# One of three wide additions a unit by an accumulating DMA, and VectorE's order in a unit redone

## The chip, the cores and the metric

The kernel runs on one core of one Trainium2 chip. The metric is the device time of one execution in microseconds; the median of several executions is compared. TensorE multiplies matrices, VectorE and ScalarE work element by element, GpSimd and SyncE (SP) here mostly issue DMAs. Lines such as L427 are lines of the kernel before.

## The reference

A layer-normalised input `x` (2048 tokens of 512) goes two ways: through attention with 32 heads over cached keys and values of 2048 positions, and through a small network B that gates the result. What matters here is the attention:

```python
q = (xn @ wq).reshape(B, Sq, H, Dh)                  # H = 32, Dh = 128, Sq = 2048
scores = einsum("bhqd,bhkd->bhqk", q, k_cache) * Dh ** -0.5
p = softmax(scores, axis=-1)
o = einsum("bhqk,bhkd->bhqd", p, v_cache)
s = o.reshape(B, Sq, H * Dh) @ wo
g = silu(B_ref(xn, ...))
return x + s * g
```

The softmax needs, for every query, the sum of its 2048 exponentials. Those sums are what the change is about.

## The kernel before

The attention is cut into 128 units: 8 groups of 4 heads, 4 blocks of 512 queries, and the 4 heads within. A unit is one head and 512 queries, and it is walked through in 8 slots (`p` = 0 to 7) of two blocks of 128 keys each. The last unit, 127, is written out by hand at the end. The order on every engine is the program's order (`pin`); nothing is moved by a scheduler. The main loop runs over slots, `n = 8 u + p`; one pass over `p` for a given `u` is called the body of unit `u` here.

- `s_slot` (L405): two score matmuls into a PSUM tile `ps_s` and one exponential of 128x1024 on ScalarE (L416) into half of a tile `pT`. A unit fills four `pT` tiles of 128x2048 (pT[0] to pT[3]) in bf16. Six such buffers exist.
- `pv_slot` (L437) multiplies `pT` with the values into `ps_o`, ten slots behind the scores; there are two buffers of `ps_o`.
- The sums over keys: VectorE adds the four `pT` tiles, keys still on partitions. `add_first` (L419, slot 4) makes acc = pT[0] + pT[1]; `add_next` (L425) adds pT[2] in slot 6 and pT[3] in slot 0 of the next body. These are the three wide additions of 128x2048. `fold` (L429) and `fold_last` (L433) halve acc twice, to 128x512.
- `turn` (L458, slot 3 of the next body) transposes acc by a DMA on SP's queue into `tT`, so that queries lie on partitions. `turned_sums` (L462, slot 0 of the body after that) reduces `tT` on VectorE, takes the reciprocal, and issues the DMA `dr` to DRAM; `bcast` (L471, slot 1) issues the DMA `rb`, which reads `dr` and spreads it over all partitions.
- `norm` (L476), called by `norm_queue` in slot 7 of the body two units later, multiplies `ps_o` by `rb` on VectorE into `oT`; this frees `ps_o`.
- `wo_mm` and `wo_post` (L500, L533) multiply `oT` with the output weights into the one bank `ps_wo` and add it to `sacc` on VectorE (L549; in the last group also L558 and L560).
- For units 16 to 123 the query projection is made for two heads at once by seven products instead of eight (`product`, L363; `q_part`, L383). `q_part` reads the products from the one bank `ps_q` on VectorE, in slots 3 and 6, and TensorE's next products into the bank come after it.

SP's queue issues, in this order within a body, `dr`, `rb`, `turn`, and then the loads of keys (`load_k`), values (`load_v`) and weights for later groups. GpSimd computes only small statistics before the attention starts and issues no DMA.

Of the kernel before, what the change touches and what calls it, by code (L numbers as in the profile page):

```python
# [9 lines left out]
ALU = mybir.AluOpType  # L10
FP32 = mybir.dt.float32
BF16 = mybir.dt.bfloat16
# [5 lines left out]
def kernel(  # L18
# [15 lines left out]
    nc = tc.nc  # L34
    P = nc.NUM_PARTITIONS
# [26 lines left out]
    pin = tc.keep_in_program_order  # L62

    def pool(name, bufs=1, space=None, **kw):
        if space is not None:
            kw["space"] = space
        return tc.tile_pool(name=name, bufs=bufs, **kw)
# [43 lines left out]
    def mm(out, lhsT, rhs, start, stop, **kw):  # L111
# [9 lines left out]
        out=ident[:], in0=diag[:], scalar1=0.0, scalar2=None, op0=ALU.is_equal))  # L121
# [6 lines left out]
    NU = len(units)  # L128
    TURN = range(NU - HG)
    NS = NU * SPU  # L130
    kTs, vBs, wqs, wos, oTs, st = {}, {}, {}, {}, {}, {}
# [183 lines left out]
    def q_mm(u, dcs, tag="xa"):  # L315
        g, qt, hh = units[u]
        if dcs[0] == 0:
            st[u] = dict(psq=psX.tile([P, 512], FP32, tag=tag, name="ps_q"))
        for dc in dcs:
            mm(st[u]["psq"][:], wqs[g * HG + hh][:, dc, :],  # L320
               xnT[:, dc, qt * 512:(qt + 1) * 512], dc == 0, dc == DC - 1)
# [83 lines left out]
    def s_slot(u, p):  # L405
        g, qt, hh = units[u]
        s = st[u]
        sps = psS.tile([P, 2, 512], FP32, name="ps_s")
        for j in range(2):
            kc = 2 * p + j  # L410
            kv = kTs[g * HG + hh].rearrange("d (i p j) -> d i j p", p=P, j=KJ)
            mm(sps[:, j, :], kv[:, kc // KJ, kc % KJ, :], s["qT"][:], True, True)
        if p % 2 == 0:
            s.setdefault("pT", []).append(pB.tile([P, 4, 512], BF16, tag="pT", bufs=6, name="pT"))
        jj = 2 * (p % 2)
        pin(nc.scalar.activation(  # L416
            out=s["pT"][-1][:, jj:jj + 2, :], in_=sps[:], func=ACT.Exp, scale=SCALE))

    def add_first(u):  # L419
        s = st[u]  # L420
        s["acc"] = pB.tile([P, 4, 512], BF16, tag="acc", bufs=2, name="acc")
        pin(nc.vector.tensor_tensor(  # L422
            out=s["acc"][:], in0=s["pT"][0][:], in1=s["pT"][1][:], op=ALU.add))

    def add_next(u, i):  # L425
        a = st[u]["acc"]
        pin(nc.vector.tensor_tensor(out=a[:], in0=a[:], in1=st[u]["pT"][i][:], op=ALU.add))  # L427

    def fold(u):  # L429
        a = st[u]["acc"]  # L430
        pin(nc.vector.tensor_tensor(out=a[:, 0:2, :], in0=a[:, 0:2, :], in1=a[:, 2:4, :], op=ALU.add))  # L431

    def fold_last(u):  # L433
        a = st[u]["acc"]
        pin(nc.vector.tensor_tensor(out=a[:, 0, :], in0=a[:, 0, :], in1=a[:, 1, :], op=ALU.add))  # L435
# [22 lines left out]
    def turn(u):  # L458
        st[u]["tT"] = pB.tile([P, 4, P], BF16, tag="tT", bufs=2, name="tT")
        pin(nc.sync.dma_start_transpose(out=st[u]["tT"][:], in_=st[u]["acc"][:, 0, :]))  # L460

    def turned_sums(u):  # L462
        s = st[u]
        sm = smp.tile([P, 4], FP32, name="sm")
        pin(nc.vector.tensor_reduce(out=sm[:], in_=s["tT"][:], axis=mybir.AxisListType.X, op=ALU.add))  # L465
        rc = smp.tile([P, 4], FP32, name="rc")
        pin(nc.vector.reciprocal(out=rc[:], in_=sm[:]))
        s["dr"] = drp.tile([P, 4], FP32, name="dr")
        pin(nc.sync.dma_start(out=s["dr"][:], in_=rc[:]))

    def bcast(u):  # L471
        st[u]["rb"] = pB.tile([P, 512], FP32, tag="rb", bufs=2, name="rb")
        pin(nc.sync.dma_start(
            out=st[u]["rb"][:], in_=st[u]["dr"][:].rearrange("p j -> (p j)").partition_broadcast(P)))

    def norm(u):  # L476
        g, qt, hh = units[u]
        s = st.pop(u)
        if hh == 0:
            oTs[(g, qt)] = pB.tile([P, HG, 512], BF16, tag="oT", bufs=2, name="oT")  # L480
        o, rb, to = s["o"][:], s["rb"][:], oTs[(g, qt)][:, hh, :]
        if u in TURN:
            o = o.rearrange("k (j p) -> k p j", j=4)
            rb, to = (x.rearrange("k (p j) -> k p j", j=4) for x in (rb, to))
        pin(nc.vector.tensor_tensor(out=to, in0=o, in1=rb, op=ALU.mult))  # L485
# [23 lines left out]
    def fin_load(t):  # L509
        xl = token(False, "xl")  # L510
        pin(nc.sync.dma_start(out=xl[:], in_=xsrc[t]))
        fin[t] = xl
# [16 lines left out]
    def pay():  # L529
        while owed:  # L530
            y_out(*owed.popleft(), nc.sync)
# [276 lines left out]
    pB = left.enter_context(pool("pB", reuse_waits="tile"))  # L808
# [40 lines left out]
    def pv_run(n):  # L849
        while pv_at[0] <= n - LAG:  # L850
            pv_slot(*divmod(pv_at[0], SPU))
            pv_at[0] += 1

    def norm_queue(u):
        norm(u)
        gg, qq, hh = units[u]
        if hh == HG - 1:
            wo_todo.extend((gg, 4 * qq + ts) for ts in range(4))
            if gg == NG - 1 and qq not in LATE:
                fin_load(4 * qq)  # L860

    UA, UB = NU - 2, NU - 1

    def wo_slot(part, n, each=2, **kw):
        gg, t = wo_todo[0]
        if part < HG // each:
            wo_mm(gg, t, tuple(range(part * each, (part + 1) * each)), **kw)
            return
        wo_todo.popleft()
        wo_post(gg, t, n)  # L870
        if gg == NG - 1 and t % 4 < 3 and t + 1 not in fin and t // 4 not in LATE:
            fin_load(t + 1)

    FIRST, LAST = 16, NU - 4
    pairs = range(FIRST, LAST + 1, 2)
    q_plan = defaultdict(list)
    steps = defaultdict(list)
    for v in pairs:
        a = (v - 2) * SPU
# [5 lines left out]
    def run_steps(n, which):  # L885
        for fn, v, k in steps.get(n, ()):
            if fn is which:
                fn(v, k)
# [4 lines left out]
    for h in range(HG, H, 2):  # L893
        u = (h // HG) * QT * HG + (-4, -2)[h % HG // 2]
# [8 lines left out]
    for n in range(UB * SPU):  # L903
        u, p = divmod(n, SPU)
        extra = len(wo_todo) > 1 and u in (2 * HG, 2 * HG + 1)
        if p == 0 and wo_box:
            wo_slot(4, n, each=1)
        s_slot(u, p)
        pv_run(n)
        for v, dcs in q_plan.get(n, ()):  # L910
            q_mm(v, dcs)
        run_steps(n, product)
        if p == 0 and u - 2 in TURN:
            turned_sums(u - 2)
        if p == 1 and u - 2 in TURN:
            bcast(u - 2)
        if p == 0 and 1 <= u:
            add_next(u - 1, 3)
            fold(u - 1)
            if u != UA:  # L920
                fold_last(u - 1)
        if p == 3 and u - 1 in TURN:
            turn(u - 1)
        if p == 0:
            twice = extra
        if twice and p < 3:
            wo_slot(p, n, tag="xa")
        for v, k in ((u + 1, 3), (u + 2, 7)):
            if p == k and "psq" in st.get(v, ()) and (k == 3) == (v > FIRST):
                q_copy(v)  # L930
        if p == 3:
            run_steps(n, q_part)
        if u - 2 in TURN:
            norm_p, sum_p, wo_p, each = 7, 5, 3, 1
        else:
            norm_p, sum_p, wo_p, each = 4, 5, 4, 1
        at_wo = [wo_p + i for i in range(HG // each + 1)]
        if FIRST - 2 <= u < LAST:
            at_wo = ([0, 3, 4, 6, 7], [0, 2, 3, 6, 7], [3, 4, 5, 6, 7], [0, 2, 3, 6, 7])[u % 4]
        if p == norm_p and 2 <= u and not u - 2 in TURN:  # L940
            norm_queue(u - 2)
        if p == sum_p and 1 <= u and u - 1 not in TURN:
            sums(u - 1)
        if p == sum_p + 1 and 1 <= u and u - 1 not in TURN:
            bcast(u - 1)
        if u == UA and p in (1, 2, 3):
            wo_slot(p - 1, n)
            if p == 3:
                fold_last(u - 1)
        if p in at_wo and wo_todo and pS is not None and (p == at_wo[0] or wo_box):  # L950
            wo_slot(at_wo.index(p), n, each=each)
        if p == norm_p and u - 2 in TURN:
            norm_queue(u - 2)
        if p != 3:
            run_steps(n, q_part)
        if p == 4:
            add_first(u)
        if p == 6:
            add_next(u, 2)
        pay()  # L960
        held_mm(n)
        for fn in todo.pop(n, ()):
            fn()
        if pS is None and not held:
            right.close()
            pS = right.enter_context(pool("pS", side="right", reuse_waits="tile"))
# [31 lines left out]
    def pv_to(k):  # L998
# [29 lines left out]
        out=diag[:], in0=diag[:], scalar1=0.0, scalar2=None, op0=ALU.is_equal))  # L1028
# [98 lines left out]
```

## Time and profile before

| | |
|---|---|
| Median of 3 runs | 1245.1 us (1244.51 to 1245.75) |
| The profiled execution | 1244.64 us, of which the span is 1242.8 us |
| Granted TensorE clock | 1.000 |
| Busy: TensorE matmul | 1230.5 us, 99% of the span |
| Busy: VectorE | 1081.4 us, 87% |
| Busy: ScalarE | 1092.2 us, 88% |
| Busy: GpSimd | 26.8 us, 2% |
| DMA share of the SP queue | 40.9% of 16 engines |

The span runs from the first to the last instruction; the execution's own time is 1.8 us more. A busy share is an average over stages with different limits, so a change in one stage is read from that stage: from the wait that ends last in it. In the groups of instructions, a line gives engine, operation, output <- input, shapes and count, then the busy time in us and the mean length of one in ns, then the idle time just before them with what ended it. In the timeline, a line gives start and length in us.

### The profile page before, as it was taken

Reading aid. Unit: us, or ns where it says so; the run is one execution under the profiler, and the core shown is the slowest. Engines: PE = TensorE matmul, PEld = TensorE weight load, DVE = VectorE, ACT = ScalarE, POOL = GpSimd, SP = SyncE. Lnnn points to the kernel's source line nnn. Section 1 sums busy time; section 2 is a strip of 40 time slices with the busy share of each in tenths; the row PEclk is TensorE's granted clock in tenths of the full one; section 3 lists DMA queues with packets and bytes.
Section 4 is the critical chain, followed back from the end, with each engine's and each line's share of the span. In section 5 each row is a group of like instructions: output and inputs, shape, how many; then the busy total and the mean of one; then the engine's idle time right before and its main releaser. Section 6 shows DMA issues by size and latency. Waiting matters only on the chain.

```text
span 1242.8 us, 17421 instructions
## 1 busy us (share of the span) xinstructions
PE 1230.5 (99%) x6267; PEld 645.0 (52%) x6267; DVE 1081.4 (87%) x1745; ACT 1092.2 (88%) x1127; POOL 26.8 (2%) x75
## 2 busy tenths in 40 slices
PE   9999999999999999999999999999999999999898
PEld 7444444455555555555555555555555555555445
DVE  7712778899999999999999999999999999999997
ACT  6345999899999999999999999999999999999886
POOL 5300000000000000000000000000000000000000
PEclk9999999999999999999999999999999999999999
DMA  7660123554334524443244423453354433563322
GB/s 176 169 138 31 30 39 65 100 97 88 69 73 106 108 47 85 91 111 77 63 96 98 94 60 82 94 117 61 66 103 94 90 69 74 104 114 68 68 73 82
DMA packets 244055, 107.74 MB, mean 87 GB/s; under 512 B 194816, under 2 KB 227712, under 8 KB 243968
## 3 DMA queue, kind: packets, MB, share of 16 engines
q1 hardware_dynamic: 243408, 106.17, 40.9%
q8 instruction: 49, 0.80, 0.3%
q10 hardware_dynamic: 560, 0.46, 0.1%
q14 instruction: 38, 0.31, 0.1%
HBM read 67.50 MB, written 2.36 MB: 56 GB/s over the span
## 4 chain that ended last, share of the span: by engine, by line
PE 86%; DVE 11%; DMA 2%; ACT 1%; issue 1%; SPq 0%; DVEq 0%; ACTq 0%
PE ps_s L112 35%; PE ps_o L112 33%; PE ps_q L112 7%; PE ps_wo L112 7%; DVE acc L427 3%; PE ps_m L112 2%; DVE oT L485 1%; DVE acc L431 1%; DMA rb<-dr 1%; DVE sm L465 1%; ACT pT L416 1%; DVE sacc L549 1%; DVE xall L558 1%; DVE acc L422 1%; DVE acc L435 1%
## 5 line engine op out<-in xcount | busy, mean ns | idle before, releaser
L416 ACT ACTIVATE pT<-ps_s 128x1024 bf16<-128x1024 f32 x1016 | 1019.7, 1024 | 77.0 <-PE ps_s L112 41.6
L112 PE MATMUL ps_s<-qT,kT 128*128 128x512 bf16 (+1 forms) x2064 | 609.1, 377 | 0.0
L112 PE MATMUL ps_o<-pT,vb 128*128 128x512 bf16 x1984 | 589.9, 379 | 0.0
L427 DVE TENSOR_TENSOR acc<-acc,pT 128x2048 bf16<-128x2048 bf16 x254 | 306.9, 1208 | 11.5 <-ACT pT L416 11.2
L112 PEld LDWEIGHTS <-kT 128*128 128x128 bf16 x2064 | 232.9, 113 | 147.3 <-issue 2.1
L112 PEld LDWEIGHTS <-vb 128*128 128x128 bf16 x1984 | 193.9, 98 | 216.9 <-issue 0.3
L112 PE MATMUL ps_wo<-wo_h,oT 128*128 128x512 bf16 x496 | 186.2, 379 | 0.1
L422 DVE TENSOR_TENSOR acc<-pT 128x2048 bf16<-128x2048 bf16 x127 | 154.8, 1219 | 20.4 <-ACT pT L416 20.1
L431 DVE TENSOR_TENSOR acc<-acc 128x1024 bf16<-128x1024 bf16 x127 | 87.9, 692 | 4.3
L485 DVE TENSOR_TENSOR oT<-ps_o,rb 128x512 bf16<-128x512 f32 x127 | 86.7, 683 | 1.8 <-DMA rb<-dr 1.5
L112 PEld LDWEIGHTS <-oT 128*128 128x128 bf16 x528 | 59.1, 112 | 49.5 <-issue 0.6
L465 DVE TENSOR_REDUCE sm<-tT 128x4 f32<-128x512 bf16 x124 | 84.0, 678 | 0.7 <-DMA tT<-acc 0.7
L549 DVE TENSOR_TENSOR sacc<-ps_wo,sacc 128x512 f32<-128x512 f32 x108 | 73.9, 685 | 0.3 <-PE ps_wo L112 0.3
L112 PEld LDWEIGHTS <-wc 128*128 128x128 bf16 x440 | 43.0, 98 | 58.4 <-issue 8.1
L112 PEld LDWEIGHTS <-wq_h 128*128 128x128 bf16 x398 | 38.9, 98 | 47.9 <-issue 1.8
L112 PE MATMUL ps_q<-xnT,wq_h 128*128 128x256 bf16 (+1 forms) x288 | 61.1, 298 | 1.6 <-DVE tq L389 1.3
L400 DVE TENSOR_TENSOR qT<-ps_q,tq 128x512 bf16<-128x512 f32 x55 | 38.1, 692 | 25.4 <-PE ps_q L112 25.1
L435 DVE TENSOR_TENSOR acc<-acc 128x512 bf16<-128x512 bf16 x127 | 54.0, 425 | 4.3
L293 ACT ACTIVATE h2T<-ps_s 128x1024 bf16<-128x1024 f32 x28 | 28.7, 1025 | 25.9 <-PE ps_s L112 25.9
L112 PEld LDWEIGHTS <-w_sb 128*128 128x128 bf16 x368 | 33.7, 98 | 29.5
L112 PE MATMUL ps_s<-xn2T,w_sb 128*128 128x512 bf16 x224 | 48.8, 379 | 0.0
L112 PE MATMUL ps_q<-xs,wc 128*128 128x256 bf16 x246 | 47.0, 273 | 0.0
(99 smaller groups left out, 574.9 us busy)
## 6 DMA issues: line engine op xcount, KB each, us to landing
rb<-dr SPq DMA_DIRECT2D x127, 256.0 KB, 3.9
vb<-in_A_v_cache_dram SPq DMA_DIRECT2D x62, 256.0 KB, 3.0
wq_h<-in_A_wq_dram SPq DMA_DIRECT2D x32, 128.0 KB, 3.1
wo_h<-in_A_wo_dram SPq DMA_DIRECT2D x32, 128.0 KB, 2.9
w_sb<-in_B_w_dram SPq DMA_DIRECT2D x8, 256.0 KB, 5.0
kT<-in_A_k_cache_dram SPq DMA_TRANSPOSE x128, 2.8
xl<-in_A_x_dram SPq DMA_DIRECT2D x16, 128.0 KB, 2.5
dr<-rc SPq DMA_DIRECT2D x127, 2.0 KB, 1.4
```

The costliest lines, as they stand in the source:

```text
L112: pin(nc.tensor.matmul(out=out, lhsT=lhsT, rhs=rhs, start=start, stop=stop, **kw))
L293: pin(nc.scalar.activation(out=h2[c, f][:], in_=ps[:], func=ACT.Gelu_apprx_tanh))
L400: pin(nc.vector.tensor_tensor(out=s["q"][:, 1:3, :], in0=ps[:], in1=s["u"][:].unsqueeze(1).to_broadcast([P, 2, 256]), op=ALU.add))
L416: pin(nc.scalar.activation(out=s["pT"][-1][:, jj:jj + 2, :], in_=sps[:], func=ACT.Exp, scale=SCALE))
L422: pin(nc.vector.tensor_tensor(out=s["acc"][:], in0=s["pT"][0][:], in1=s["pT"][1][:], op=ALU.add))
L427: pin(nc.vector.tensor_tensor(out=a[:], in0=a[:], in1=st[u]["pT"][i][:], op=ALU.add))
L431: pin(nc.vector.tensor_tensor(out=a[:, 0:2, :], in0=a[:, 0:2, :], in1=a[:, 2:4, :], op=ALU.add))
L435: pin(nc.vector.tensor_tensor(out=a[:, 0, :], in0=a[:, 0, :], in1=a[:, 1, :], op=ALU.add))
L465: pin(nc.vector.tensor_reduce(out=sm[:], in_=s["tT"][:], axis=mybir.AxisListType.X, op=ALU.add))
L485: pin(nc.vector.tensor_tensor(out=to, in0=o, in1=rb, op=ALU.mult))
L549: pin(nc.vector.tensor_tensor(out=sa, in0=ps[:], in1=sa, op=ALU.add))
L558: pin(nc.vector.scalar_tensor_tensor(out=gl, in0=sa, scalar=0.5, in1=gl, op0=ALU.mult, op1=ALU.mult))
```

## The change

For units 14 to 119 (`BY_DMA`, 106 of them) the first wide addition leaves VectorE. A second accumulator tile `accB` is filled by two DMAs: in slot 1 SP's queue copies pT[0] into it (`copy_first`, 512 KB within SBUF), and in slot 3 GpSimd's queue adds pT[1] to it by an accumulating DMA (`add_second`, 512 KB). VectorE makes acc = pT[2] + pT[3] in slot 0 of the next body (`add_first` with i = 2), and then adds `accB` to it (`add_both`). So two wide additions are left on VectorE. The tag `acc` has three buffers instead of two.

The order on VectorE in slot 0 becomes: `norm` of three units back (before: two units back, in slot 7), pT[2] + pT[3], the reduction and the reciprocal, `add_both`. The two folds go from slot 0 to slot 3, behind `q_part`, and `turn` goes from slot 3 to slot 4, so that on SP's queue it stands behind the copy of that body. The order of TensorE and ScalarE is as before. GpSimd's queue has 106 accumulating DMAs and nothing else in the attention. In the last of the changed bodies, that of unit 120, VectorE has two wide additions of unit 119 and two of unit 120 by the old order.

```diff
--- before.py
+++ after.py
@@ -416,11 +416,24 @@
         pin(nc.scalar.activation(
             out=s["pT"][-1][:, jj:jj + 2, :], in_=sps[:], func=ACT.Exp, scale=SCALE))
 
-    def add_first(u):
+    def add_first(u, i=0):
         s = st[u]
-        s["acc"] = pB.tile([P, 4, 512], BF16, tag="acc", bufs=2, name="acc")
+        s["acc"] = pB.tile([P, 4, 512], BF16, tag="acc", bufs=3, name="acc")
         pin(nc.vector.tensor_tensor(
-            out=s["acc"][:], in0=s["pT"][0][:], in1=s["pT"][1][:], op=ALU.add))
+            out=s["acc"][:], in0=s["pT"][i][:], in1=s["pT"][i + 1][:], op=ALU.add))
+
+    def copy_first(u):
+        s = st[u]
+        s["accB"] = pB.tile([P, 4, 512], BF16, tag="acc", bufs=3, name="acc")
+        pin(nc.sync.dma_start(out=s["accB"][:], in_=s["pT"][0][:]))
+
+    def add_second(u):
+        s = st[u]
+        pin(nc.gpsimd.dma_start(out=s["accB"][:], in_=s["pT"][1][:], accum_op=ALU.add))
+
+    def add_both(u):
+        a = st[u]["acc"]
+        pin(nc.vector.tensor_tensor(out=a[:], in0=a[:], in1=st[u]["accB"][:], op=ALU.add))
 
     def add_next(u, i):
         a = st[u]["acc"]
@@ -872,6 +885,7 @@
             fin_load(t + 1)
 
     FIRST, LAST = 16, NU - 4
+    BY_DMA = range(14, NU - 8)
     pairs = range(FIRST, LAST + 1, 2)
     q_plan = defaultdict(list)
     steps = defaultdict(list)
@@ -910,16 +924,23 @@
         for v, dcs in q_plan.get(n, ()):
             q_mm(v, dcs)
         run_steps(n, product)
+        if p == 0 and u - 3 in BY_DMA:
+            norm_queue(u - 3)
+        if p == 0 and u - 1 in BY_DMA:
+            add_first(u - 1, 2)
         if p == 0 and u - 2 in TURN:
             turned_sums(u - 2)
         if p == 1 and u - 2 in TURN:
             bcast(u - 2)
         if p == 0 and 1 <= u:
-            add_next(u - 1, 3)
-            fold(u - 1)
-            if u != UA:
-                fold_last(u - 1)
-        if p == 3 and u - 1 in TURN:
+            if u - 1 in BY_DMA:
+                add_both(u - 1)
+            else:
+                add_next(u - 1, 3)
+                fold(u - 1)
+                if u != UA:
+                    fold_last(u - 1)
+        if p == 3 + (u - 1 in BY_DMA) and u - 1 in TURN:
             turn(u - 1)
         if p == 0:
             twice = extra
@@ -930,6 +951,9 @@
                 q_copy(v)
         if p == 3:
             run_steps(n, q_part)
+            if u - 1 in BY_DMA:
+                fold(u - 1)
+                fold_last(u - 1)
         if u - 2 in TURN:
             norm_p, sum_p, wo_p, each = 7, 5, 3, 1
         else:
@@ -949,13 +973,18 @@
                 fold_last(u - 1)
         if p in at_wo and wo_todo and pS is not None and (p == at_wo[0] or wo_box):
             wo_slot(at_wo.index(p), n, each=each)
-        if p == norm_p and u - 2 in TURN:
+        if p == norm_p and u - 2 in TURN and u - 2 not in BY_DMA:
             norm_queue(u - 2)
         if p != 3:
             run_steps(n, q_part)
-        if p == 4:
+        if u in BY_DMA:
+            if p == 1:
+                copy_first(u)
+            if p == 3:
+                add_second(u)
+        elif p == 4:
             add_first(u)
-        if p == 6:
+        elif p == 6:
             add_next(u, 2)
         pay()
         held_mm(n)
```

## The prediction

> **What bounds the kernel now.** I read the page first, then the windows view, then the timeline of one unit.
>
> ```profile
> span 1242.8 us, 17421 instructions
> ...
> PE 1230.5 (99%) x6267; PEld 645.0 (52%) x6267; DVE 1081.4 (87%) x1745; ACT 1092.2 (88%) x1127; POOL 26.8 (2%) x75
> ...
> PE 86%; DVE 11%; DMA 2%; ACT 1%; issue 1%; SPq 0%; DVEq 0%; ACTq 0%
> ```
>
> TensorE is busy for 1230.5 of 1242.8 us and carries 86% of the chain that ended last. VectorE, which the change relieves, has 11% of the chain. Where that 11% lies decides what the relief is worth, so the windows come next.
>
> ```profile
> core 0: us, PE busy (x) PEld busy (x) DVE busy (x) ACT busy (x) POOL busy (x), PEclk, DMA share, GB/s
> 250.00:300.00 50.00, 49.65 (x248) 25.82 (x246) 47.97 (x80) 46.05 (x47) 0.00 (x0) 1.00 0.59 106
> ...
> 600.00:650.00 50.00, 50.00 (x254) 26.39 (x253) 46.00 (x72) 47.33 (x48) 0.00 (x0) 1.00 0.39 89
> ```
> ```profile
> 1100.00:1156.00 56.00, 54.01 (x271) 28.18 (x269) 52.96 (x83) 50.37 (x51) 0.00 (x0) 1.00 0.45 84
> 1156.00:1200.00 44.00, 39.88 (x195) 20.33 (x194) 42.17 (x69) 37.18 (x38) 0.00 (x0) 1.00 0.34 70
> ```
>
> In the middle TensorE is full (50.00 of 50.00) at full clock while VectorE has 46.00, so VectorE's work is covered there. TensorE loses 0.35 us between 250 and 300, 1.99 us between 1100 and 1156, and 4.12 us between 1156 and 1200, where VectorE is at 42.17 of 44. Only those small losses can come back. Units 14 to 119 are changed. Eight exponentials make a unit, so unit 120 begins with the 961st, which counted through the timeline is the fourth of this row's nine:
>
> ```profile
> 1153.21 9.45 ACT L416 ACTIVATE pT<-ps_s 128x1024 bf16<-128x1024 f32 x9 [1.55 <-PE ps_s L112]
> ```
>
> That is 1153.21 + 3 x 1.05 = 1156.4: the 4.12 us lie behind the changed stage.
>
> How long is one unit?
>
> ```profile
> 599.69 16.85 ACT L416 ACTIVATE pT<-ps_s 128x1024 bf16<-128x1024 f32 x16 [0.22 <-PE ps_s L112]
> 616.76 13.55 ACT L416 ACTIVATE pT<-ps_s 128x1024 bf16<-128x1024 f32 x13 [0.22 <-PE ps_s L112]
> 630.65 2.96 ACT L416 ACTIVATE pT<-ps_s 128x1024 bf16<-128x1024 f32 x3 [0.33 <-PE ps_s L112]
> 633.83 16.84 ACT L416 ACTIVATE pT<-ps_s 128x1024 bf16<-128x1024 f32 x16 [0.22 <-PE ps_s L112]
> ```
>
> From 599.69 to 633.83 are 32 exponentials, four units: 34.14 / 4 = 8.53 us a unit, set by TensorE.
>
> **The change, part by part.**
>
> *Removed from VectorE:* one wide addition in each of 106 units.
>
> ```profile
> L427 DVE TENSOR_TENSOR acc<-acc,pT 128x2048 bf16<-128x2048 bf16 x254 | 306.9, 1208 | 11.5 <-ACT pT L416 11.2
> ...
> L422 DVE TENSOR_TENSOR acc<-pT 128x2048 bf16<-128x2048 bf16 x127 | 154.8, 1219 | 20.4 <-ACT pT L416 20.1
> ```
>
> At 1.21 us each that is 128 us of VectorE time, and nothing on the path while TensorE is full. What it can return is the 0.35 and 1.99 us above, and perhaps a quarter of the 4.12, where VectorE would enter the end with less behind it: 2.3 to 3.3 us.
>
> *Added: two transfers in a row, with a wait behind them.* In unit k's body SP issues the copy of pT[0], after the broadcast `rb`. GpSimd's accumulate of pT[1] waits for the copy to land. In body k+1 VectorE's `add_both` waits for the accumulate. Queued behind `add_both` are `q_part`, both folds, the evacuation of `ps_wo` and the normalisation; for `q_part` TensorE waits (one bank `ps_q`), for the fold waits `turn`, for `turn` the reduction of body k+2, and for its reciprocal SP's `dr`, `rb` and so the next copy. That is a ring over two units. Its fixed parts stand in the timeline of one unit (start, length, engine, line), then in two rows of SP's queue, then among the DMA issues (count, KB each, median us from issue to landing):
>
> ```profile
> 607.60 0.68 DVE L465 TENSOR_REDUCE sm<-tT 128x4 f32<-128x512 bf16 x1
> ...
> 608.31 0.18 DVE L467 RECIPROCAL rc<-sm 128x4 f32<-128x4 f32 x1
> ...
> 608.41 1.19 DVE L427 TENSOR_TENSOR acc<-acc,pT 128x2048 bf16<-128x2048 bf16 x1
> ...
> 608.52 0.33 SPq L469 DMA_DIRECT2D dr<-rc  x1
> ...
> 609.63 0.69 DVE L431 TENSOR_TENSOR acc<-acc 128x1024 bf16<-128x1024 bf16 x1
> ...
> 609.93 0.33 SPq L473 DMA_DIRECT2D rb<-dr  x1
> ...
> 610.36 0.43 DVE L435 TENSOR_TENSOR acc<-acc 128x512 bf16<-128x512 bf16 x1
> ...
> 610.70 0.42 DVE L388 COPY tq<-ps_q 128x256 f32<-128x256 f32 x1
> ...
> 610.82 1.20 SPq L460 DMA_TRANSPOSE tT<-acc  x1
> ...
> 611.15 0.42 DVE L389 TENSOR_TENSOR tq<-ps_q,tq 128x256 f32<-128x256 f32 x1
> ```
> ```profile
> 601.54 0.32 SPq L473 DMA_DIRECT2D rb<-dr  x1
> 601.96 1.19 SPq L460 DMA_TRANSPOSE tT<-acc  x1
> ```
> ```profile
> rb<-dr SPq DMA_DIRECT2D x127, 256.0 KB, 3.9
> vb<-in_A_v_cache_dram SPq DMA_DIRECT2D x62, 256.0 KB, 3.0
> ...
> dr<-rc SPq DMA_DIRECT2D x127, 2.0 KB, 1.4
> tT<-acc SPq DMA_TRANSPOSE x124, 3.7
> ...
> out_dram<-xl SPq DMA_DIRECT2D x12, 128.0 KB, 1.7
> ...
> w_sb<-in_B_w_dram SPq DMA_DIRECT2D x1, 512.0 KB, 5.5
> ```
>
> From the start of a reciprocal: `dr` is issued 0.21 us later (608.31 to 608.52), `rb` 1.41 after that (it waits for `dr` to land), and SP's next DMA 0.42 after `rb` (601.54 to 601.96): the copy goes out at +2.04. Then come C, the copy from issue to landing, and A, the accumulate. Then a wide addition (608.41 to 609.63, 1.22), two steps of `q_part` (610.70 to 611.57, 0.87), two folds (609.63 to 610.79, 1.16) and 0.03 to the issue of `turn`: 3.28. `turn` lands in 3.7, and the reduction takes 0.71 up to the next reciprocal (607.60 to 608.31). The ring is 2.04 + C + A + 3.28 + 3.7 + 0.71 = 9.73 + C + A, and it spans two units, 17.07 us at TensorE's pace. So **C + A up to 7.3 us is free; above that each unit takes (9.73 + C + A) / 2.**
>
> *C.* No row is a plain copy within SBUF. From below: the stores, SBUF to DRAM, take 1.4 us for 2 KB and 1.7 for 128 KB; that slope, an estimate, gives 512 KB 1.2 us above the fixed 1.4: 2.6. From above: `rb` stands right ahead on the same queue and lands at 3.9; the copy's 1.2 us of moving behind it gives 3.9 - 0.42 + 1.2 = 4.7. `rb` is ahead every time, so I take 4.4.
>
> *A.* No row shows an addition by DMA or a DMA of GpSimd's queue. Lowest: adding costs nothing, 2.6 like the copy. Highest: the one 512 KB row (5.5 us, in the crowded start), its part above 1.4 paid twice: 5.5 + 4.1 = 9.6. An adding transfer must read source and destination, so 2.6 + 1.2 = 3.8 is the row-based middle; I add 1.0 for company, because `turn` moves at the same time and the same transpose has this spread:
>
> ```profile
> DMA to landing us min/median/max: 3.4/3.7/5.8
> ```
>
> So A = 4.8. The company is real: the queue (packets, MB, share of the 16 engines) already has 40.9%, and the two transfers add at least (1.2 + 2.4) / 8.53 = 42% of a unit.
>
> ```profile
> q1 hardware_dynamic: 243408, 106.17, 40.9%
> ```
>
> The Trainium skill's "DMA: Bandwidth & Descriptors" (Anatomy of one DMA — SWDGE path) prices a DMA from GpSimd at about 2.0 us plus its bytes at 436 GB/s, 3.2 us here; by that both transfers come to 6.4 us and the ring is free, which is the first rival below. Its "Collectives: The Full Stack" (The bandwidth ceiling) speaks against the change: a reducing transfer reads two sources on one ring and measured half the rate of a copy, between DRAM buffers; by that the accumulate is an estimated 4.4 us, and with my C the sum is 8.8 and the unit 9.27. No run before shows either.
>
> *Sum.* C + A = 9.2; a unit takes (9.73 + 9.2) / 2 = 9.47 instead of 8.53, +0.93. Over 105 units (the first of the 106 has no ring behind it) that is +98 us; the lost 2 us around 1100 to 1156 vanish in it. The profiled run took 1244.6 us (span 1242.8), 0.5 below the median of 1245.1: 1244.6 + 98 - 2 = **1340 us**.
>
> *Moved, at no cost by themselves.* The normalisation goes from slot 7 to slot 0 of the next body; on VectorE it still follows the `ps_wo` evacuation, so its real place stays, and `rb` has a slot more to land. If that cover went, TensorE's slot 2 would wait for `ps_o`, 0.7 us a unit. The additions of pT[2] and pT[3] now stand ahead of the reduction and so delay `dr`, `rb` and the copy by 1.22; nothing else reads `rb` until the next body. `turn` moves behind the copy on SP; the weight and cache loads behind it start later, with units to spare. GpSimd's queue is empty then (POOL 0.00 above).
>
> **The rivals.**
>
> *1. The transfers fit: faster.* With C = 2.6 and A = 3.8, C + A is 6.4, below the 7.3 from which it decides. TensorE keeps 8.53 us a unit and returns 2.3 to 3.3 us: 1241.6. For it: the stores' slope; against it: `rb` right ahead, and 40.9% of the engines taken. Chance 0.18.
>
> *2. Hidden anyway: no change.* The transfers fit, but the end is limited by units 120 on, unchanged, and body 120 holds four wide additions (two of unit 119, two of its own) instead of three, which eats the gain: 1244. Chance 0.06.
>
> *3. The adding itself is slow.* With A = 9.6 the unit is (9.73 + 4.4 + 9.6) / 2 = 11.87, +3.33: 1593 us. For it: nothing shows the rate of additions; against it: the 5.5 is from the crowded start. All C + A above 11.2 belong here, chance 0.12.
>
> **How the numbers follow.** The forecast's own case is C + A from 7.4 to 11.2, chance 0.64: 1244 to 1445 us, around 1340. A measurement of this kernel can tell about 0.2%, 2.5 us, from no change. Faster 0.18 (rival 1), same 0.06 (rival 2), slower 0.76. The range has to take in rival 1, so it begins at 1240; it ends at 1440, leaving out the last of the forecast's case and rival 3, under 2 in 10 together.
>
> **What would show it.** Right: behind the accumulate the wide addition waits on a DMA in nearly every unit, `ps_q` matmuls wait for VectorE, sixteen exponentials span some 18.9 us instead of 17.07, TensorE's windows fall to about 45 of 50, copy and accumulate land in about 4.4 and 4.8 us. Wrong: 50.00 of 50.00 in the middle with no DMA wait on VectorE (rival 1 or 2), or an accumulate near 10 us (rival 3). If copy and accumulate land as priced and the unit is still 8.53 us, my ring is wrong. If the landing of `turn` or `rb` doubles, the fixed part of the ring was too small.

## The result, and the profile after

The changed kernel takes 1576.5 us (median of four runs, 1573.7 to 1577.5) against 1244.8 us for the kernel before on the same chip: 1.266 times as long, with a 95% interval of 1.264 to 1.268. The forecast was 1340 us in a range of 1240 to 1440. The direction was right, the size was not: instead of +95 us it is +332 us. The profiled execution took 1573.7 us.

The page of the changed kernel: span, busy times, the two DMA queues (packets, MB, share of the 16 engines) and the chain that ended last.

```profile
span 1572.0 us, 17794 instructions
...
PE 1330.3 (85%) x6267; PEld 666.1 (42%) x6267; DVE 976.2 (62%) x1639; ACT 1092.9 (70%) x1127; POOL 118.9 (8%) x181
...
q1 hardware_dynamic: 258672, 161.75, 42.4%
q0 software_dynamic: 15264, 55.58, 19.6%
...
PE 38%; DMA 36%; DVE 17%; ACT 5%; issue 3%; SPq 1%; POOLq 0%; ACTq 0%; DVEq 0%
```

VectorE has indeed lost its work (1081.4 to 976.2 us), but TensorE fell from 99% to 85% of the span and from 86% to 38% of the chain. DMAs took its place, 36% of the chain where they had 2%.

The windows of the changed kernel, the same middle stretch as before:

```profile
core 0: us, PE busy (x) PEld busy (x) DVE busy (x) ACT busy (x) POOL busy (x), PEclk, DMA share, GB/s
600.00:650.00 50.00, 42.47 (x196) 21.13 (x194) 31.55 (x57) 36.36 (x37) 3.48 (x4) 0.93 0.68 159
```

In 50 us there are 37 exponentials instead of 48, and no engine is full: that is a stage held up by waits. Which waits? The table of waits of the changed kernel (us in total, times, longest):

```profile
ACT pT L416 <- PE ps_s L112: 378.5, 278, 6.8
...
DVE acc L436 <- DMA acc<-pT: 285.6, 102, 5.3
PE ps_q L112 <- DVE qT L398: 210.3, 55, 6.0
...
DVE sm L478 <- DMA tT<-acc: 17.0, 20, 1.7
...
DVE oT L498 <- DMA rb<-dr: 13.6, 23, 1.4
```

VectorE's `add_both` (L436 now) waits for the accumulate in 102 of 106 units, 2.8 us each. Behind it on VectorE is `q_part` (L398), and TensorE waits 55 times for that. ScalarE's wait for scores only follows from TensorE's. The turned sums and `rb` are hardly waited for. The order in which this happens in one unit stands in the timeline of the changed kernel (start, length, engine, line; in brackets the idle time before and what ended it):

```profile
745.67 1.23 DVE L422 TENSOR_TENSOR acc<-pT 128x2048 bf16<-128x2048 bf16 x1 [0.20 <-ACT pT L416]
...
746.82 0.68 DVE L478 TENSOR_REDUCE sm<-tT 128x4 f32<-128x512 bf16 x1
746.84 0.87 POOL L432 DMA_DIRECT2D acc<-pT  x1 [10.77 <-ACT pT L416]
...
747.53 0.18 DVE L480 RECIPROCAL rc<-sm 128x4 f32<-128x4 f32 x1
747.73 0.33 SPq L482 DMA_DIRECT2D dr<-rc  x1
751.43 1.23 DVE L436 TENSOR_TENSOR acc<-acc 128x2048 bf16<-128x2048 bf16 x1 [3.73 <-DMA acc<-pT]
751.60 0.33 SPq L486 DMA_DIRECT2D rb<-dr  x1
752.03 0.48 SPq L428 DMA_DIRECT2D acc<-pT  x1
...
753.03 0.42 DVE L398 TENSOR_TENSOR qT<-ps_q,tq 128x256 bf16<-128x256 f32 x1
...
753.50 0.59 PE L112 MATMUL ps_q<-xnT,wc 128*128 128x256 bf16 x2 [3.09 <-DVE qT L398]
...
754.54 1.20 SPq L473 DMA_TRANSPOSE tT<-acc  x1
754.98 1.02 ACT L416 ACTIVATE pT<-ps_s 128x1024 bf16<-128x1024 f32 x1 [3.89 <-PE ps_s L112]
...
757.45 0.87 POOL L432 DMA_DIRECT2D acc<-pT  x1 [9.73 <-DMA tT<-acc]
```

The accumulate issued at 746.84 ends VectorE's wait at 751.43. Into the same 4.6 us falls `dr`, issued at 747.73: 2 KB, and `rb`, which waits for it, goes out only at 751.60, 3.9 us later (before: 1.41). The copy follows at 752.03, and its accumulate at 757.45. So the accumulate of one unit holds back the `dr` of another unit, and through `rb` and the copy the next accumulate.

The DMA issues of the changed kernel (KB each, median us to landing):

```profile
acc<-pT SPq DMA_DIRECT2D x106, 512.0 KB, 4.6
acc<-pT POOLq DMA_DIRECT2D x106, 512.0 KB, 5.0
rb<-dr SPq DMA_DIRECT2D x127, 256.0 KB, 3.8
...
dr<-rc SPq DMA_DIRECT2D x127, 2.0 KB, 3.0
tT<-acc SPq DMA_TRANSPOSE x124, 3.5
```

Copy and accumulate land in 4.6 and 5.0 us, close to the 4.4 and 4.8 of the forecast; `rb` and `turn` are no slower than before. `dr` went from 1.4 to 3.0.

The ring of the prediction, its steps measured: each is the mean over units 18 to 117 of the distance from the start of one instruction to the start of the next, taken from the trace's instruction records. The sum equals two unit periods by construction (unit by unit 11.66 us), so the table shows where the time sits, not yet what causes it.

| step (us) | forecast | after |
|---|---|---|
| reduction to reciprocal | 0.71 | 0.72 |
| reciprocal to `dr` | 0.21 | 0.26 |
| `dr` to `rb` | 1.41 | 3.41 |
| `rb` to copy | 0.42 | 0.48 |
| copy to the accumulate's issue (C) | 4.4 | 5.34 |
| accumulate's issue to `add_both` (A) | 4.8 | 5.07 |
| `add_both` to `turn` | 3.28 | 3.19 |
| `turn` to reduction | 3.7 | 4.89 |
| sum, two units | 18.9 | 23.3 |

The excess of 4.4 us over two units is 2.2 a unit, and 105 x 2.2 = 232 us on top of 1340 gives 1572, as it must.

Which links of the ring hold? In the same records, over units 20 to 112, the copy is issued within 0.8 us of `rb` in all 93 units, and `add_both` starts within 0.1 us of the accumulate's landing in 91. But the reduction starts within 0.1 us of the landing of `turn` in only 34. In the other 59 VectorE comes to it later: ahead of it stands pT[2] + pT[3], which in each of them waits for an exponential (as in the 745.67 line), so for the pace of TensorE, which `add_both` holds up through `q_part`. So the delay comes back by two ways, over `turn` and over TensorE.

### The profile page after: what moved, and what is told of

Read it like the earlier page. It is cut to its first block, busy times and chain, and to the rows that moved or that the text cites. A ratio compares the mean times of both kernels' runs of the same rounds, so it can differ in the third digit from the quotient of the medians.

```text
span 1572.0 us, 17794 instructions
## 1 busy us (share of the span) xinstructions
PE 1330.3 (85%) x6267; PEld 666.1 (42%) x6267; DVE 976.2 (62%) x1639; ACT 1092.9 (70%) x1127; POOL 118.9 (8%) x181
## 3 DMA queue, kind: packets, MB, share of 16 engines
q0 software_dynamic: 15264, 55.58, 19.6%
## 4 chain that ended last, share of the span: by engine, by line
PE 38%; DMA 36%; DVE 17%; ACT 5%; issue 3%; SPq 1%; POOLq 0%; ACTq 0%; DVEq 0%
DMA acc<-pT 28%; PE ps_s L112 16%; PE ps_o L112 13%; DMA dr<-rc 5%; PE ps_q L112 5%; DVE acc L436 5%; ACT pT L416 4%; PE ps_wo L112 2%; DVE acc L422 2%; DMA rb<-dr 2%; PE ps_m L112 2%; DMA tT<-acc 2%; DVE qT L398 1%; DVE sm L478 1%; DVE acc L440 1%
## 5 line engine op out<-in xcount | busy, mean ns | idle before, releaser
L112 PE MATMUL ps_s<-qT,kT 128*128 128x512 bf16 (+1 forms) x2064 | 649.5, 399 | 0.0
L112 PE MATMUL ps_o<-pT,vb 128*128 128x512 bf16 x1984 | 625.8, 399 | 0.0
L112 PEld LDWEIGHTS <-kT 128*128 128x128 bf16 x2064 | 240.1, 117 | 166.6 <-issue 17.8
L436 DVE TENSOR_TENSOR acc<-acc 128x2048 bf16<-128x2048 bf16 x106 | 129.8, 1224 | 285.6 <-DMA acc<-pT 285.6
L112 PEld LDWEIGHTS <-vb 128*128 128x128 bf16 x1984 | 202.4, 102 | 246.2 <-issue 49.7
L112 PE MATMUL ps_q<-xnT,wc 128*128 128x256 bf16 x194 | 42.5, 306 | 210.3 <-DVE qT L398 210.3
L432 POOL DMA_DIRECT2D acc<-pT x106 | 92.4, 871 | 1336.0 <-DMA acc<-pT 451.9
L112 PE MATMUL ps_wo<-wo_h,oT 128*128 128x512 bf16 x496 | 191.7, 390 | 0.9 <-DVE sacc L562 0.9
L498 DVE TENSOR_TENSOR oT<-ps_o,rb 128x512 bf16<-128x512 f32 x127 | 86.8, 683 | 13.9 <-DMA rb<-dr 13.6
L112 PEld LDWEIGHTS <-wq_h 128*128 128x128 bf16 x398 | 43.5, 109 | 89.0 <-issue 56.8
L440 DVE TENSOR_TENSOR acc<-acc,pT 128x2048 bf16<-128x2048 bf16 x42 | 50.9, 1212 | 11.5 <-ACT pT L416 11.2
```

What stands on the lines that cost most here:

```text
L112: pin(nc.tensor.matmul(out=out, lhsT=lhsT, rhs=rhs, start=start, stop=stop, **kw))
L432: pin(nc.gpsimd.dma_start(out=s["accB"][:], in_=s["pT"][1][:], accum_op=ALU.add))
L436: pin(nc.vector.tensor_tensor(out=a[:], in0=a[:], in1=st[u]["accB"][:], op=ALU.add))
```

## The experiments

All but the last pair are single executions beside the kernel before (1244.8 to 1245.7 us); differences of tens of us are read from them, no smaller ones. Times are compared with 1576 for the changed kernel. The edits are shortened: `pin(...)` around a call is left out, and a comment stands for lines that are not shown.

**Is it one ring over two units?** First, the accumulate's result is not waited for at all:

```diff
-            in0=a[:], in1=st[u]["accB"][:]
+            in0=a[:], in1=st[u]["pT"][3][:]
```

> Both transfers run as in the changed kernel, but add_both adds pT[3] a second time instead of accB, so VectorE waits for no transfer; the sums leave out pT[0] and pT[1]. Two-unit ring (accumulate, add_both, folds, turn, reduction, dr, rb, copy): it is cut, a unit is back at 8.53 us and the time at 1242 to 1250 us. One-unit ring (dr cannot land while the accumulate of the unit before moves, rb waits for dr, the copy for rb, the next accumulate for the copy: 0.1 + 0.5 + 5.3 + 5.1 = 11.0 us): it stays, a unit takes about 11 us and the time is 1480 to 1530 us, and VectorE waits for rb. Traffic (the bytes themselves slow everything): near the changed kernel, 1500 to 1576 us.

Measured: 1521.1 us. Cutting the ring that the prediction described gains only 55 us. The wait that stands out in this run:

```profile
DVE oT L498 <- DMA rb<-dr: 353.2, 106, 7.1
```

Now VectorE waits in all 106 units for `rb`, and with that wait a shorter chain closes in one unit. Its steps (means over units 20 to 114): `dr` to `rb` 4.37 us, with an accumulate in flight at each of these `dr`; `rb` to its landing and `norm` 3.76; `norm` and pT[2] + pT[3] up to the next reduction 2.07; reduction to the next `dr` 0.97. That is 11.17 us, the unit of this run, and `norm` starts 0.02 us after `rb` has landed in each of the 95 units, so there is no slack in it. The kernel before has the same chain at 7.18 of 8.55 us, the changed kernel at 10.30 of 11.67. The way that the expectation named, over `dr`, `rb`, the copy behind it and the next accumulate, closes in one unit too and fits the same period; the runs do not part the two. Both go through the landing of `dr`, and neither needs the sum on VectorE. Does a chain of one unit alone explain the time? Then changing every second unit would be free:

```diff
-    BY_DMA = range(14, NU - 8)
+    BY_DMA = range(14, NU - 8, 2)
```

> Only every second unit uses the DMAs (53 of 106). Two-unit ring: it closes from one such unit to the next; with dr free of an accumulate (1.4 instead of 3.4 us) it is 23.3 - 2.0 = 21.3 us at most and 20 at least, against 17.07 for two units: 53 x 3 to 4.2 us, 1405 to 1470 us. One-unit ring: there is no accumulate in the unit before, so it does not close: about 1245 us. Traffic: half of the 332 us, about 1410 us.

Measured: 1465.2 us. The time alone fits the ring over two units, but the trace does not: in 47 even units the reduction never starts less than 0.68 us after `turn` has landed (1.8 on average), so this ring does not close over `turn` here. Each pass may simply be late by itself. With every third unit no ring closes:

```diff
+    BY_DMA = range(14, NU - 8, 3)
```

> Only every third unit uses the DMAs (36 of 106). Two-unit ring: two such units are three units apart, 25.6 us at TensorE's pace, so a chain of 21 to 23 us no longer closes on itself: 1242 to 1255 us. One-unit ring: does not close either, about 1245 us. Traffic: a third of the 332 us, about 1355 us.

Measured: 1377.4 us. This refutes what both ring theories expected here. 36 units cost (1377 - 1245) / 36 = 3.7 us each, the even ones (1465 - 1245) / 53 = 4.2, all of them (1576 - 1245) / 106 = 3.1. A pass through the two transfers is late even without a ring: copy to `add_both` takes 10.2 us in this run (medians of 5.4 up to the accumulate's issue, 4.7 behind it). The waits show how much of that is late:

```profile
DVE acc L436 <- DMA acc<-pT: 112.3, 36, 4.8
```

VectorE waits in all 36 units, 3.1 us each, so the slots leave some 7.1. TensorE is full, so what it loses in one such unit it can't make up in the two that follow. A ring is not needed for a loss; it can only carry the delay on. Two other costs are in the 3.7 us and were not parted from it: the body behind each such unit holds four wide additions on VectorE, and TensorE's clock is at half for 71 us of this run, which is worth 36 of the 132 us at most.

**How much is the adding?** The accumulate becomes a plain copy (pT[0] then is missing from the sums):

```diff
-        nc.gpsimd.dma_start(out=s["accB"][:], in_=s["pT"][1][:], accum_op=ALU.add)
+        nc.gpsimd.dma_start(out=s["accB"][:], in_=s["pT"][1][:])
```

> GpSimd's transfer copies pT[1] into accB instead of adding it (the sums leave out pT[0]); same queue, bytes, order and waits. If adding is what makes the transfer long and holds dr back: its 4096-byte packets take about 0.16 instead of 0.33 us, the transfer falls from 5.1 to about 3.7 us, dr to rb from 3.4 to about 2.2 us, the two-unit ring from 23.3 to about 20.7 us, a unit to 10.4 us: about 1440 us. If moving alone is the cost, not adding: within 2% of 1576 us.

Measured: 1443.4 us. Of this run, the DMA queue and the issues:

```profile
q0 software_dynamic: 15264, 55.58, 10.4%
```
```profile
acc<-pT POOLq DMA_DIRECT2D x106, 512.0 KB, 3.3
...
dr<-rc SPq DMA_DIRECT2D x127, 2.0 KB, 2.3
```

The same packets and bytes take half of the engines' time (10.4% of 1442 us against 19.6% of 1572), and land in 3.3 instead of 5.0 us. In the packet records a 4096-byte packet takes 338 ns when it adds and 159 when it copies (medians), 2.1 times. `dr` to `rb` shrinks with it, to 2.50. So adding is worth 133 of the 332 us; the other 199 a plain transfer in that place would cost too.

**Does the accumulate hold up `dr`?** Four accumulates of 128 KB, so that `dr` could pass between them:

```diff
+        for k in range(4):
+            nc.gpsimd.dma_start(out=s["accB"][:, k, :], in_=s["pT"][1][:, k, :], accum_op=ALU.add)
```

> The accumulate is issued as four DMAs of 128x512 instead of one of 128x2048. If a small DMA (dr) waits until the engines are through with the accumulate DMA that they have begun: it waits for one piece, dr to rb falls from 3.4 to about 2.1 us, the accumulate itself gets longer (four issues of about 0.87 us, some 5.5 to 6 us), together about 22.7 us over two units: 1520 to 1560 us. If dr waits for all of the accumulate's bytes whatever their cut: dr to rb stays at 3.4 or more and the time rises over 1576 us.

Measured: 1675.4 us. `dr` to `rb` fell from 3.41 to 2.35, as expected, but the accumulate's step rose from 5.07 to 7.69. In this run's timeline and DMA issues:

```profile
623.01 3.56 POOL L433 DMA_DIRECT2D acc<-pT  x4 [5.36 <-DMA acc<-pT]
```
```profile
acc<-pT POOLq DMA_DIRECT2D x424, 128.0 KB, 4.1
```

GpSimd spends 3.56 / 4 = 0.89 us on each issue, and the last of the four lands 7.0 us after the first was begun (mean; the 4.1 of the row is the median of all 424). In the packet records (medians), the first 16-byte packet of `dr` starts 0.82 us after its issue where nothing is in its way, 2.54 while a whole accumulate moves, 1.51 while the plain copy of the run before does, 1.21 among the quarters, although these move on for about 4 us more. So `dr` does not wait for the whole series. Whether it would also pass a quarter that already stands in the queue is not shown: the next one is issued only 0.89 us later. The page shows 15264 / 106 = 144 packets a transfer, 9 on each of 16 engines; by the medians the 8 that carry data take 8 x 0.338 = 2.7 us when adding, 1.3 as a copy, 0.9 in a quarter (107 ns each), and the extra waits (1.7, 0.7, 0.4) stay below these and fall in that order. The Trainium skill's "DMA: Bandwidth & Descriptors" (Queues, rings and completion order) says that an engine takes turns between queues, but drains a whole packet, typically 9 to 17 descriptors, before it switches. If the 9 are what that page calls one packet, the waits are such as its rule would give.

**The `dr` ring cut.** `rb` reads the `dr` of the unit before (wrong normalisers, everything moves); alone, and with the cut of the first experiment:

```diff
+        dr = drs[u - 1] if u in BY_DMA and u - 1 in BY_DMA else drs[u]
-            in_=st[u]["dr"][:].rearrange(...)
+            in_=dr[:].rearrange(...)
```

> The changed kernel, but rb of a changed unit reads the dr of the unit before, which has landed long ago, so SP issues rb and the copy without waiting for the new dr (each unit is normalised with its neighbour's sums). All transfers remain. Two-unit ring with dr's landing taken out: 23.3 - 3.4 + 0.4 = 20.3 us, 10.2 a unit: about 1418 us (1390 to 1450). If the bytes and not the wait for dr set the time: 1540 to 1576 us.

Measured: 1447.5 us; `dr` to `rb` is 0.50 here. And with both cuts:

> Both cuts together: add_both adds pT[3] a second time instead of accB, and rb reads the dr of the unit before; copies and accumulates all move, nobody waits for them but the buffers. If the two waits are the cause: no chain is left, 1243 to 1290 us against 1521 with the first cut alone. If the moving bytes are the cause: 1450 us or more.

Measured: 1270.2 us. The windows view of this run:

```profile
250.00:1150.00 900.00, 875.87 (x4308) 460.54 (x4393) 707.68 (x1191) 817.79 (x818) 88.88 (x102) 1.00 0.90 203
```

Every byte still moves, the DMA engines are at 0.90 and 203 GB/s, and TensorE is back at 97% and full clock. So the time goes to the two waits, for the accumulate's sum and for `dr`, not to the traffic as such. One cut takes off 55 us, the other 129, both together 306: either wait alone keeps the kernel slow. Where the 25 us that are left come from was not tested.

**Orders that might lift the waits.** `rb` a slot later, so that the copy no longer stands behind it on SP's queue:

```diff
-        if p == 1 and u - 2 in TURN:
+        if p == 1 + (u - 2 in BY_DMA) and u - 2 in TURN:
             bcast(u - 2)
```

> For the changed units the broadcast rb is issued one slot later, so SP issues the copy before it and the copy no longer waits for dr to land. Ring of the copy behind dr: dr to rb (3.4 us) leaves the ring and the copy has no rb ahead of it (5.3 to about 4.1 us until the accumulate's issue); 23.3 falls to about 18.7 us over two units, 9.35 a unit: about 1330 us (1300 to 1380). If not the ring but the moving bytes set the time: within 3% of 1576 us, since they are the same.

Measured: 1414.7 us, a gain of 162 but less than expected. The DMA issues of this run show one reason:

```profile
acc<-pT SPq DMA_DIRECT2D x106, 512.0 KB, 3.2
acc<-pT POOLq DMA_DIRECT2D x106, 512.0 KB, 5.5
```

The copy lands in 3.2 instead of 4.6 us, but the accumulate now meets `rb` and takes 5.5. The waits show a second reason: `norm` waits for the later `rb`, 60.6 us in all where the changed kernel had 13.6. Next, `add_both` moved to slot 3, behind `q_part`, so that TensorE's wait for `ps_q` goes:

> add_both stands behind q_part on VectorE (slot 3, ahead of the folds), so q_part and TensorE's product behind it no longer wait for the accumulate. Ring: it still closes over turn and dr; only q_part (0.87 us) leaves it: 22.5 us over two units, about 1500 to 1540 us. If TensorE's wait for q_part behind add_both is the cause: it is gone, and the time falls under 1300 us.

Measured: 1534.6 us, as expected. The 210 us of `ps_q` waits were only the place where the delay came out. Both moves together:

> Both: rb after the copy, and add_both behind q_part. The copy goes out when its exponentials are there, about 2.6 us into its unit; with 3.6 and 5.1 us the sum is there 2.8 us into the next one, ahead of slot 3, where q_part is done at 4.2. Ring over turn: 0.7 + 0.3 + 0.4 + 4.1 + 5.1 + 2.4 + 3.7 to 4.9 = 16.7 to 17.9 us against 17.07: a unit at 8.53 to 8.95 us, 1243 to 1290 us. If the bytes set the time: within 3% of 1576 us.

Measured: 1398.5 us, far above the expectation, which had counted the chain over `turn` and not the one over `norm`. The waits of this run:

```profile
DVE oT L498 <- DMA rb<-dr: 159.3, 96, 4.3
DVE acc L436 <- DMA acc<-pT: 71.2, 64, 4.5
```

VectorE now waits longer for `rb` than for the accumulate. The steps of the first experiment's chain, `dr` to `rb` to `norm` to the next reduction and `dr`, add up to 9.96 us of a unit of 10.00 here, and `norm` starts within 0.1 us of the landing of `rb` in 93 of 95 units. The loads of keys and values seem to lengthen it: units 16 to 118 take 10.7 us on average while such loads are issued (up to 18.4) and 8.9 otherwise, with 25 of these 40 at 8.4 to 8.6 as in the kernel before. So the same kernel without most of those loads, and as a control the changed kernel without them:

```diff
+        if h >= HG:
+            kTs[h] = kTs[h % HG]     # vBs likewise
+            return
```

> As the kernel with rb after the copy and add_both behind q_part (1398 us), but the keys and values of heads 4 to 31 are not loaded (but for the last head's values): the first four heads' are used again, so the attention is that of other heads. If those loads hold up turn, dr, rb and the copies: 1243 to 1270 us. If the transfers pay by themselves: 1370 to 1400 us.

> The changed kernel with the same loads left out. Ring: its length is made of dr behind the accumulate, the copy behind rb and the accumulate itself, none of them loads: 1480 to 1576 us. If the loads are the cause there as well: under 1430 us.

Measured: 1276.4 and 1528.2 us. With the better order the loads make 122 of the remaining 153 us; in the changed kernel itself they make 48 of 332, and its waits go on without them. What the better order still loses without loads sits in the same chain:

```profile
DVE oT L504 <- DMA rb<-dr: 106.5, 92, 2.9
```

It adds up to 8.79 us of a unit of 8.83, and (8.83 - 8.53) x 105 is the 32 us by which this run exceeds the kernel before.

**Is there a version that gains?** The better order, only in units that I took to be free of loads, and only near the end:

```diff
+    BY_DMA = [v for v in range(16, NU - 16) if v % 16 in (2, 3, 4, 5, 6)]
```

> As the kernel with rb after the copy and add_both behind q_part, but only units 2 to 6 of each group of 16 use the DMAs (30 units), while no keys or values are loaded. If the loads of keys and values on the same queue and engines are what that order still pays for: nothing is paid here, 1243 to 1252 us. If each unit with the transfers pays its share whatever else moves ((1398 - 1245) / 106 = 1.45 us): about 1288 us.

Measured: 1280.4 us, 1.029 times the kernel before (1.028 to 1.031), nearer to the second expectation. The first two units of each run of five still overlap loads of keys and values, so the choice was bad. But the loads are not all of it: in each group of 16, units 3, 5, 7 and 8 take 9.8, 10.9, 9.8 and 9.4 us on average, the others 8.4 to 8.8, and no keys or values are loaded in units 5, 7 and 8. For units 2 to 4 `norm` again starts 0.02 us after `rb` lands; units 7 and 8 are the hand-over to the old order, where the body of unit 7 has four wide additions. What each of these costs was not tested.

```diff
+    BY_DMA = range(116, 123)          # and dr issued behind the copy
```

> As the kernel with rb after the copy and add_both behind q_part, with dr behind the copy too, but only units 116 to 122 use the DMAs: no keys or values are loaded there, and VectorE is the bound. If the transfers are in time: VectorE is relieved of 7 x 1.2 us where TensorE lost 6.1 us, of which 2 to 4 come back: 1241 to 1243 us, faster than the kernel before. If they are late even here (10.2 us for copy and accumulate, against some 9 that this order allows): 1247 to 1260 us.

Measured: 1250.5 us, 1.0047 times (1.0034 to 1.0061), as the second expectation had it. Even there the transfers come late: the accumulates of units 116 and 117 land 10.4 and 10.5 us after the copy's issue, VectorE waits 5.2 us for these two and 4.5 us for `rb`, and unit 121 takes 13.8 us instead of 10.6. No version tried beats the kernel before.

## Why the prediction was wrong

- *What bounds the kernel; the removed addition.* Right: VectorE gave up 105 us of busy time (128 forecast) and nothing came of it.
- *The form of the ring, two units long.* Right in part: `add_both` waits in nearly every unit, and TensorE at `ps_q`. But its link from `turn` to the reduction holds in 34 of 93 units only, and with every second unit changed in none; elsewhere the delay came back over TensorE and the exponentials. And it was taken as the only one: a chain of one unit through the landing of `dr` was not seen, and keeps 1521 us when the other is cut.
- *"Moved, at no cost by themselves."* Not so for `norm`: it stands ahead of the reduction, now with pT[2] + pT[3] between them, and waits for `rb`. In the kernel before that chain had 1.4 us to spare; next to none is left of that in the first experiment and in the better orders.
- *"`rb` 1.41 after that (it waits for `dr` to land)".* This term was mis-sized most: 3.41 us, 2.0 of the 4.4 missing. The 1.41 came from one unit; the mean of the kernel before was already 1.83 (median 1.44), and no accumulate moved there. The "company" was charged to the accumulate alone, and not to the 2 KB transfer that stands in its way.
- *"`turn` lands in 3.7" as the whole step to the reduction.* It lands in 3.5, but the step is 4.89: the reduction also has its place on VectorE behind `norm` and pT[2] + pT[3], and that waits for an exponential (the 745.67 line). 1.2 us. The prediction's own sign, a landing of `turn` or `rb` that doubles, did not come, and the fixed part was too small all the same.
- *C = 4.4.* It lands in 4.7 on average (the 4.6 above is the median); another 0.6 passes before GpSimd's issue begins. 0.9 us too little together.
- *A = 4.8.* 5.07, right to 0.3 us, and rival 3 (9.6) is refuted. The 338 against 159 ns a packet fit the rule cited from the Trainium skill's "Collectives: The Full Stack" (The bandwidth ceiling), that a transfer which reads two sources has half the rate, here between SBUF buffers; that the second read is the reason no run here shows. The 3.2 us cited from the Trainium skill's "DMA: Bandwidth & Descriptors" (Anatomy of one DMA — SWDGE path) fit the plain transfer (3.3), not the adding one (5.0).
- *"C + A up to 7.3 us is free; above that each unit takes (9.73 + C + A) / 2."* This is the step of the mechanism that failed: by it a pass that closes no ring costs nothing, but passes three units apart lose 3.7 us each (1377). The two transfers must fit between their own slots, and a full TensorE has no slack with which to repay.
- *The sum.* With the measured steps in place of the forecast's it gives 1572 us, but it must, since they add up to the period. It says that four terms were too small, by 2.0, 1.2, 0.9 and 0.3 us; it does not show that the ring set the pace.
- *Rivals 1 and 2.* They needed C + A below 7.3; the two steps are 10.4. The direction, slower, was right for the reason given: VectorE waits for the accumulate and TensorE behind it.

## What to carry to other kernels

Work moved here from a busy engine that was not the bound to DMAs gained nothing and added waits; price the whole chain from issue to issue, with every small transfer that will stand behind the large one. List all rings through a new transfer, those that had slack before and the queue's own order among them, check in the trace which links are tight, and cut the waits together when testing: one cut alone showed 55 and 129 us of a 306 us effect. Where TensorE was full, a chain that came late once was a loss, whether or not it closed on itself.

## What the runs showed of the hardware

- A 2 KB DMA on SP's queue landed in 1.4 us before and 3.0 beside the accumulates of GpSimd's queue (medians); with the accumulate cut into quarters it started after 1.2 instead of 2.5 us.
- An accumulating 512 KB DMA within SBUF took 5.0 us and a plain one in its place 3.3; GpSimd needed 0.87 us to issue an accumulating one and 0.54 for a plain one.
- TensorE at 97% went with DMA engines at 0.90 (the last cut above).
- The granted clock fell with long gaps in TensorE's work, not with idle time as such. Between 250 and 1150 us:

```profile
250.00:1150.00 900.00, 731.26 (x3330) 363.80 (x3329) 541.07 (x900) 623.07 (x620) 67.14 (x77) 0.92 0.68 153
```
```profile
250.00:1150.00 900.00, 727.59 (x3393) 364.80 (x3459) 557.70 (x939) 641.08 (x644) 69.74 (x80) 0.98 0.74 158
```

The first is the changed kernel, the second the one with the accumulate's result not waited for. TensorE is idle for 169 and 172 us, but in the matmul records the first has 40 gaps over 2 us and the second 12. In the clock records the clock is either full or half, and it is at half in 37 stretches of the first (143 us) and 8 of the second (31 us), each 3.4 us long or twice that. The Trainium skill's "TensorE: Matmul & The Clock Gate" (What's actually happening) halves the clock after an idle window of some 3.4 us. The halving and the 3.4 us agree with it, but a gap need not be that long: in the run with the plain copy the clock is at half 22 times, with 26 gaps over 2 us and only 4 over 3.4. What the lower clock itself cost was not measured apart.
